# The first loads of x and W1: six loads of 128 to 256 KB, x on one queue and W1 on the other, in place of twelve of 64 to 128 KB

## The chip, the core and the metric

One core of one Trainium2 chip runs the whole kernel. The metric is the device time of one execution in microseconds (us), lower is better. The kernel before takes 141.57 us in the median of 13 runs, 140.27 us in the fastest and 144.7 us in the slowest.

A core has a matmul engine (PE; its weight loads are listed apart as PEld), a vector engine (DVE), an activation engine (ACT), a general engine (POOL), and sixteen DMA engines that move data between DRAM and on-chip memory. A transfer is started by an instruction on a queue. This kernel uses two queues: that of SP, an engine that does nothing else, and that of ACT, whose own instructions stand in the same order as its transfers.

## The reference

A sequence x of 2048 rows by 448 columns (bf16) goes through two branches, and a gate mixes them.

```python
g = sigmoid((x * gate_w).sum(-1, keepdims=True))
# branch A: a diagonal complex state space model with 448 states
dt = exp(log_dt);  Lam_bar = exp(dt * Lam);  B_bar = ((Lam_bar - 1) / Lam)[:, None] * B
h_t = Lam_bar * h_(t-1) + B_bar @ x_t          # 2048 steps
a = 2 * real(C @ h_t) + x * Dskip
# branch B: a feed-forward layer, 448 -> 1792 -> 448
b = silu(x @ w1) @ w2
out = g * a + (1 - g) * b
```

## The kernel before

Two successive rows of x are read as one row of 896 columns, so the 2048 rows are 1024 even and 1024 odd rows. They are worked on in four chunks of 512 rows: chunk 0 and 1 hold even rows, chunk 2 and 3 odd ones. x is needed with its columns on the partitions (XT). For chunk 0, PE does the turning: `turn_x` (L487) transposes 128x128 blocks of XN into PSUM and `turned_x` (L495) has DVE copy them to XT. For the other chunks DMA transposes on the SP queue (L308 to L320) do it. 448 columns are three full blocks of 128 (j = 0, 1, 2) and a rest of 64.

W1 has 1792 columns, two halves of 896 that are worked on in pairs (c = 0 and 1). Each half is loaded in three column ranges, `CUT`: the first 384 columns, which serve the first six output blocks of chunk 0, then 256, then 256 more.

An explicit tracker (class `Tracker`) puts the instructions on each engine in the order in which the Python code calls it, and adds a semaphore wait wherever a named buffer was last written by another engine or a transfer. Every load has its own key, so a matmul waits for exactly the loads whose keys it lists, and each load counts as landed when all of its sixteen parts are. The order on each engine is fixed by hand.

The order of the loads before is below. Each x load of columns 0-255 is 64 KB (one block k of 128 rows), each W1 load of a j and a half is 96 KB.

| SP queue | ACT queue |
|---|---|
| x rows k=0, columns 0-255 | x rows k=1 |
| W1 j=0, half 0 | W1 j=0, half 1 |
| x rows k=2 | x rows k=3 |
| W1 j=1, half 0 | W1 j=1, half 1 |
| log_dt, Lambda_re (one row each) | Lambda_im, Dskip (one row each) |
| x columns 256-511, k=0,1 (128 KB) | x columns 256-511, k=2,3 (128 KB) |
| W1 j=2, half 0 | W1 j=2, half 1 |
| W1's last 64 rows, half 0 (112 KB) | the same, half 1 |
| W1 second range (192 KB), third range (192 KB), half 0 | the same, half 1 |
| DMA transposes of x and B, gate and skip rows, x, W2 (1568 KB) ... | ACT's own work |

What PE does at the start, in its order:

- 22 matmuls of ones (`warm`), then `turn_x` of j=0 and j=1 for k=0,1, then two more of ones
- `ffn1_first` (L425): six output blocks of chunk 0, one matmul at a time, j=0 for the left half of the columns, then the right half, then j=1, then j=2. It is a generator: after its fourth matmul `turn_x(0, 1)` comes, after the sixth `turn_x(1, 1)`, and after the second of j=1 `mm_cols` (L467), which turns the four parameter rows R0 to R3 into columns. DVE prepares these with `rd` (L463), and copies the result to PV, from which all the scan's coefficients come. Then the turning of j=2 and 3 follows, and the other eight matmuls of `ffn1_first`.
- `ffn1_rem` (L441): the 64 rest columns, three pairs of matmuls. ACT applies silu.
- from then on `pair` (helper `lanes`, L361 to L370, matmul at L366): two 64-row matmuls side by side, for W1's other columns, the other chunks and the input projection of the scan (BT, BR). The first such pair is output blocks 6 and 7 of chunk 0, which reads both halves of W1's second range.

Later, the scan needs the half-swap of a tile over partitions: `VE<-VE`, two transfers on the SP queue (L938). They stand behind the load of W2 there. DVE's L842 reads them, and PE waits for that result. `XR` (copies of the 64 rest columns to the other half of the partitions, `swap_xr`, L236) is written by DVE when the transposed odd rows of x have landed.

Of the kernel before, what the change touches and what calls it, by code (L numbers as in the profile page):

```python
# [151 lines left out]
def gated_mix(nc, A_x, A_Lambda_re, A_Lambda_im, A_B_re, A_B_im, A_C_re, A_C_im, A_log_dt,  # L152
              A_Dskip, B_x, B_w1, B_w2, gate_w, out):
    with ExitStack() as ctx:
        E = ctx.enter_context
        T = Tracker(nc, ctx)

        def sb(name, shape, dtype):
            return E(nc.sbuf_tensor(name, list(shape), dtype))
# [5 lines left out]
        W1E = sb("W1E", [128, 4, F_FF], BF16)  # L165
# [24 lines left out]
        ID = sb("ID", [128, 128], BF16)  # L190
# [31 lines left out]
        ps = E(nc.psum_tensor("ps", [128, 8, 512], F32))  # L222
# [3 lines left out]
        def ld(eng, dst, src, key, group=None):  # L226
            return T.dma(eng, lambda e: e.dma_start(dst, src), writes=[key], group=group)  # L227
# [24 lines left out]
            return v.rearrange("(o n) -> o n", o=1)  # L252

        XH = XN[:, 0:8 * D].rearrange("p (k c) -> p k c", k=4)
        XA = ["XA0", "XA1", "XA2", "XA3", "XB0", "XB1"]
        HF = F_FF // 2
        CUT = ((0, 384), (384, 640), (640, HF))
        x0 = x2[0:512, 0:512].rearrange("(k p) c -> p k c", p=128)

        def ld_x(eng, k):  # L260
            ld(eng, XH[:, k, 0:256], x0[:, k, 0:256], XA[k])

        def ld_w(eng, j, c):
            f = slice(HF * c, HF * c + CUT[0][1])
            ld(eng, W1E[:, j, f], B_w1[j * 128:(j + 1) * 128, f], f"W1Ej{j}{c}")

        def ld_row(eng, i, v):
            ld(eng, R[i:i + 1, 0:D], row(v), f"R{i}", gR if i < 2 else gR2)
# [5 lines left out]
        def ld_wr(eng, c, f0, f1, key):  # L274
            ld(eng, W1E[64 * c:64 * c + 64, 3, f0:f1], B_w1[384:448, HF * c + f0:HF * c + f1], f"W1Er{key}{c}")

        for k, eng in enumerate(("sp", "act")):
            ld_x(eng, k)
        ld_w("sp", 0, 0)
        ld_w("act", 0, 1)  # L280
        for k, eng in ((2, "sp"), (3, "act")):
            ld_x(eng, k)
        ld_w("sp", 1, 0)
        ld_w("act", 1, 1)
        for i, (eng, v) in enumerate((("sp", A_log_dt), ("sp", A_Lambda_re), ("act", A_Lambda_im), ("act", A_Dskip))):
            ld_row(eng, i, v)
        for i, eng in enumerate(("sp", "act")):
            ld(eng, XH[:, 2 * i:2 * i + 2, 256:512], x0[:, 2 * i:2 * i + 2, 256:512], XA[4 + i])
        for c, eng in enumerate(("sp", "act")):
            ld_w(eng, 2, c)  # L290
        for c, eng in enumerate(("sp", "act")):
            ld_wr(eng, c, 0, HF, "")
        for c, eng in enumerate(("sp", "act")):
# [18 lines left out]
        for i, src in enumerate((A_B_re, A_B_im)):  # L312
# [17 lines left out]
             writes=["IOTA"])  # L330
# [9 lines left out]
        def nxt():  # L340
            n_bank[0] += 1
            return BANKS[(n_bank[0] - 1) % len(BANKS)]
# [56 lines left out]
        def ff(fb):  # L399
            return fb // 2 + NFB // 2 * (fb % 2)  # L400

        def wj(fb):
            i, c = fb // 2, fb % 2
            return [f"W1Ej{j}{c}" for j in range(3)] if i < 3 else [f"W1E1{c}"] if i < 5 else [f"W1E2{c}"]

        def w1(fb):
            return lambda p, j: W1E[p, j, ff(fb) * 128:(ff(fb) + 1) * 128] if j < 3 else \
# [10 lines left out]
        def ffn1_pair(c, fb, p=None):  # L418
            odd, h = c // 2, c % 2
            banks = at(p) if p is not None else [nxt(), nxt()]  # L420
            return (*[(banks[i], odd, h, w1(fb + i)) for i in range(2)],
                    wj(fb) + wj(fb + 1) + (XO if odd else XE)[h][0], rem_ffn1(odd, h, fb),
                    lambda: ffn1_act(c, fb, banks[0], 2))

        def ffn1_first():  # L425
            banks = [nxt() for _ in range(NF1)]
            for j, h in ((0, 0), (0, 1), (1, None), (2, None)):
                c = slice(0, 512) if h is None else slice(256 * h, 256 * h + 256)
                for n, fb in enumerate((0, 2, 4, 1, 3, 5)):
                    bank = banks[fb]  # L430
                    T.op("pe", lambda pe, fb=fb, bank=bank, j=j, h=h, c=c: pe.matmul(
                        ps[:, bank, c], W1E[:, j, ff(fb) * 128:(ff(fb) + 1) * 128], XT[:, j, c],
                        start=(h == 0), stop=(h == 0), skip_group_check=(h != 0)),
                        reads=[f"W1Ej{j}{fb % 2}"] + (
                            ["XTe02"] if j == 2 else [f"XTe0{j}{h}"] if h is not None else [f"XTe0{j}0", f"XTe0{j}1"]),
                        writes=[f"ps{bank}"])
                    if (j, h, n) in ((0, 0, 3), (0, 0, 5), (1, None, 1), (1, None, 3)):
                        yield
            yield banks
# [16 lines left out]
        def ffn1(c, f0=0, ahead=None):  # L456
            for fb in range(f0, NFB, 2):
                pair(*ffn1_pair(c, fb))
                if ahead and fb == 8:
                    ahead()  # L460
                yield
# [22 lines left out]
        PB = (6, 7, 6, 7)  # L484
        xp = [ps[:, b, 0:256].bitcast(BF16) for b in PB]

        def turn_x(j, i):  # L487
            def mm(pe):
                ins = None
                for k in (2 * i, 2 * i + 1):  # L490
                    ins = pe.transpose(xp[j][:, k * 128:(k + 1) * 128], XH[:, k, j * 128:(j + 1) * 128], ID[:, :])
                return ins
            T.op("pe", mm, reads=(XA[2 * i:2 * i + 2] if j < 2 else [XA[4 + i]]) + ["ID"], writes=[f"ps{PB[j]}"])

        def turned_x(j, i=None):  # L495
            c, key = (slice(0, 512), f"XTe0{j}") if i is None else (slice(256 * i, 256 * i + 256), f"XTe0{j}{i}")
# [2 lines left out]
        for j in range(2):  # L499
            turn_x(j, 0)  # L500
            turned_x(j, 0)
        warm(2, 5)
        first = ffn1_first()
        next(first)
        turn_x(0, 1)
        turned_x(0, 1)
        next(first)
        turn_x(1, 1)
        turned_x(1, 1)
        rd()  # L510
# [4 lines left out]
            reads=["ps7"], writes=["PV"])  # L515
# [37 lines left out]
        for j in (2, 3):  # L553
# [12 lines left out]
            reads=["f2"] + SGN, writes=["f2s"])  # L566
# [6 lines left out]
             reads=["li"] + SGN, writes=["lis"])  # L573
# [42 lines left out]
        def xblock(b):  # L616
            v = XN[:, 4 * b * D:4 * (b + 1) * D].rearrange("p (k c) -> p k c", k=4) if b > 1 else \
                XH[:, :, b * D:(b + 1) * D]
            return v, [*(XA if b < 2 else []), *([f"XN{b // 2}"] if b else [])]

# [12 lines left out]
        def skip():  # L633
            for b in range(4):
# [16 lines left out]
             writes=["BTz"] + BTK[2:4])  # L651
# [455 lines left out]
        f = ffn1(2)  # L1107
# [75 lines left out]
def bass_gated_mix__ssm_conv_s5__dense_activation_silu__prompt_kernel(nc, *args):  # L1183
    gated_mix(nc, *args)
# [28 lines left out]
```

## Time and profile before

The profiled execution took 141.06 us: a span of 139.3 us from the first instruction to the last, and 1.76 us around it. The median of the runs (141.57 us) is 0.51 us above it.

| | |
|---|---|
| profiled execution | 141.06 us |
| its span | 139.3 us |
| PE busy | 133.4 us, 96% |
| DVE busy | 114.7 us, 82% |
| ACT busy | 93.7 us, 67% |
| POOL busy | 13.6 us, 10% |
| moved by DMA | 11.94 MB, mean 86 GB/s |

When the first loads were issued and when they had landed, from the trace's records of each load's semaphore (us from the span's start; first and last of the sixteen parts):

| load | SP: issued, landed | ACT: issued, landed |
|---|---|---|
| x k=0 / k=1 | 0.79, 2.37 to 2.81 | 0.79, 2.57 to 2.98 |
| W1 j=0 | 1.23, 3.10 to 3.61 | 1.25, 3.44 to 3.84 |
| x k=2 / k=3 | 1.71, 3.68 to 4.16 | 1.74, 3.89 to 4.33 |
| W1 j=1 | 2.17, 4.39 to 5.06 | 2.22, 4.66 to 5.26 |
| two parameter rows | 2.65, 5.80 (last) | 2.71, 5.99 (last) |
| x columns 256-511 | 3.30, 5.33 to 6.80 | 3.59, 5.76 to 7.27 |
| W1 j=2 | 3.76, 6.14 to 7.54 | 4.03, 6.43 to 8.06 |
| W1 last 64 rows | 4.26, 6.87 to 8.32 | 4.56, 7.17 to 9.32 |
| W1 second range | 4.88, 8.45 to 10.90 | 5.12, 9.09 to 11.35 |
| W1 third range | 5.50, 9.68 to 12.27 | 5.86, 12.12 to 12.54 |

How to read the profile: a line of the timeline gives start, duration, engine, source line, operation, output<-input, and in brackets how long the engine had been idle before it and what ended that. A line of the chain gives start, duration and what the last work of the kernel was waiting for at that time. Line 366 and line 227 are helpers: all pair matmuls and all plain loads carry them.

### The profile page before, as it was taken

How to read it: one execution, taken by the hardware profiler on the slowest of the kernel's cores; microseconds unless marked ns; L12 is line 12 of the kernel's file. 1: busy time of each engine (PE TensorE's matmuls, PEld its weight loads, DVE VectorE, ACT ScalarE, POOL GpSimd, SP SyncE). 2: the span in 40 equal slices, each digit the busy share in tenths (PEclk: the TensorE clock that was granted, in tenths of full speed). 3: DMA queues.
4: the chain of work that ended last, by engine and by line, in shares of the span. 5: the costliest groups of instructions: out<-in, count | busy, mean ns of one | idle time of the engine just before them, and what ended most of it. 6: DMA issues, size and time to landing. Idle time of an engine off the chain costs nothing.

```text
span 139.3 us, 2417 instructions
## 1 busy us (share of the span) xinstructions
PE 133.4 (96%) x963; PEld 66.8 (48%) x963; DVE 114.7 (82%) x150; ACT 93.7 (67%) x146; POOL 13.6 (10%) x32
## 2 busy tenths in 40 slices
PE   7997999989997999999999999999999999999992
PEld 7633555533442555444445544444555555555552
DVE  1389979338469999999999999999999999990563
ACT  0387699797948995199997997697312536879200
POOL 7119086004000000000000000000000000000000
DMA  4999956998988440000023000000000000222123
GB/s 110 230 255 184 159 109 85 234 157 291 375 197 151 102 92 0 0 5 0 18 57 80 0 0 0 0 5 0 0 0 0 0 5 0 99 91 74 66 99 99
DMA packets 25681, 11.94 MB, mean 86 GB/s; under 512 B 16580, under 2 KB 25160, under 8 KB 25672
## 3 DMA queue, kind: packets, MB, share of 16 engines
q1 hardware_dynamic: 23652, 10.70, 33.8%
q10 hardware_dynamic: 2020, 1.11, 3.0%
q8 instruction: 7, 0.11, 0.4%
q14 instruction: 2, 0.02, 0.0%
HBM read 5.51 MB, written 1.84 MB: 53 GB/s over the span
## 4 chain that ended last, share of the span: by engine, by line
PE 77%; DMA 10%; ACT 5%; ACTq 3%; DVE 2%; SPq 1%; issue 1%
PE ps L366 32%; PE ps L773 31%; PE ps L995 15%; DMA VE<-VE 5%; DMA W1E<-in_B_w_dram 4%; ACTq L227 3%; ACT ps L806 2%; ACT VE L804 1%; DVE HS L842 1%; ACT ps L825 1%; SPq L938 1%; ACT VE L822 1%; ACT AT L453 1%; DVE TMPS L1019 1%
## 5 line engine op out<-in xcount | busy, mean ns | idle before, releaser
L773 PE MATMUL ps<-W,AT 128*128 128x448 bf16 x224 | 42.9, 353 | 0.0
L366 PE MATMUL ps<-XT,W1E 64*128 64x512 bf16 x325 | 40.1, 377 | 2.0 <-DMA W1E<-in_B_w_dram 1.1
L453 ACT ACTIVATE AT<-ps 128x1024 bf16<-128x1024 f32 x28 | 28.2, 1018 | 12.0 <-PE ps L366 11.9
L773 PEld LDWEIGHTS ps<-W,AT 128*128 128x128 bf16 x224 | 21.6, 98 | 21.2 <-issue 0.4
L366 PEld LDWEIGHTS ps<-XT,W1E 64*128 64x128 bf16 x325 | 17.4, 94 | 21.1 <-DMA W1E<-in_B_w_dram 1.5
L366 PE MATMUL ps<-XT,BT 64*128 64x512 bf16 x156 | 20.4, 377 | 0.1
L786 ACT ACTIVATE BT<-ps,GT 128x448 bf16<-128x448 f32 x8 | 5.1, 633 | 13.1 <-PE ps L773 13.1
L366 PEld LDWEIGHTS ps<-XT,BT 64*128 64x128 bf16 x156 | 8.3, 94 | 9.3 <-DVE HS L842 0.6
L842 DVE SCALAR_TENSOR_TENSOR HS<-VE,P,ps 128x512 bf16<-128x512 bf16 (+1 forms) x13 | 9.6, 781 | 3.1 <-PE ps L366 1.9
L886 DVE TENSOR_TENSOR_SCAN G<-P,Q 128x1024 f32<-128x1024 f32 (+1 forms) x6 | 11.4, 1922 | 0.0
L995 PE MATMUL ps<-CO,VE 128*128 128x448 bf16 (+2 forms) x63 | 11.1, 332 | 0.0
L995 PE MATMUL ps<-CO,HS 128*128 128x448 bf16 x56 | 11.1, 353 | 0.0
L366 PE MATMUL ps<-XR,W1E 64*128 64x512 bf16 x25 | 9.3, 377 | 0.0
L995 PEld LDWEIGHTS ps<-CO,VE 128*128 128x128 bf16 x63 | 6.0, 98 | 4.8
L995 PEld LDWEIGHTS ps<-CO,HS 128*128 128x128 bf16 x56 | 5.5, 98 | 5.1
L839 DVE TENSOR_TENSOR Q<-G,COS 128x2048 bf16<-128x2048 f32 (+1 forms) x4 | 7.0, 1756 | 0.1
L804 ACT ACTIVATE VE<-ps 128x1024 bf16<-128x1024 f32 x6 | 6.1, 1018 | 1.4 <-PE ps L366 1.3
L839 DVE TENSOR_TENSOR Q<-G,SIN 128x2048 bf16<-128x2048 f32 (+1 forms) x4 | 7.0, 1752 | 0.0
L806 ACT ACTIVATE ps<-VE,P 128x1024 f32<-128x1024 bf16 x6 | 6.7, 1119 | 0.2
L842 DVE SCALAR_TENSOR_TENSOR VE<-HS,P,FP 128x512 bf16<-128x512 bf16 (+1 forms) x7 | 6.6, 977 | 0.1
L1019 DVE SCALAR_TENSOR_TENSOR OT<-ps,GT,BT 128x448 bf16<-128x448 f32 x4 | 2.6, 682 | 4.8 <-PE ps L995 4.8
L842 DVE SCALAR_TENSOR_TENSOR FP<-HS,P,VE 128x1024 f32<-128x1024 bf16 (+1 forms) x4 | 6.2, 1550 | 0.1
(120 smaller groups left out, 169.8 us busy)
## 6 DMA issues: line engine op xcount, KB each, us to landing
W<-in_B_w_dram SPq DMA_DIRECT2D x1, 1568.0 KB, 10.7
XN<-in_A_x_dram SPq DMA_DIRECT2D x1, 896.0 KB, 5.7
out_dram<-OT SPq DMA_DIRECT2D x8, 112.0 KB, 1.7
out_dram<-TMPS SPq DMA_DIRECT2D x7, 112.0 KB, 1.7
HS<-HS SPq DMA_DIRECT2D x4, 128.0 KB, 2.5
W1E<-in_B_w_dram SPq DMA_DIRECT2D x2, 192.0 KB, 6.4
W1E<-in_B_w_dram ACTq DMA_DIRECT2D x2, 192.0 KB, 6.5
XN<-in_A_x_dram SPq DMA_DIRECT2D x1, 384.0 KB, 6.6
```

The costliest lines, as they stand in the source:

```text
L227: return T.dma(eng, lambda e: e.dma_start(dst, src), writes=[key], group=group)
L366: ins = pe.matmul(ps[:, bank, :], w(p, j), xh(odd, h, j, p), start=start and j == js[0], stop=stop and j == js[-1], skip_group_check=seeded)
L453: T.op("act", lambda e: e.activation(a[:, fb:fb + n, :], ps[:, bank:bank + n, :], AF.Silu), reads=[f"ps{bank + i}" for i in range(n)], wri ...
L773: ins = pe.matmul(ps[:, bank, 0:D], a[:, fb, q * 128:(q + 1) * 128], W2[:, ff(fb), :], start=(first and fb == 0), stop=(fb == NFB - 1), sk ...
L786: T.op("act", lambda e: e.activation(bs(tile), ps[:, bank, 0:D], AF.Copy, scale=sc), reads=[f"ps{bank}", "GT2" if h else "GRI"], writes=ks)
L804: T.op("act", lambda e: e.activation(VE[:, m:m + 2, hs], ps[:, b[0]:b[0] + 2, :], AF.Copy), reads=[f"ps{i}" for i in b], writes=vs)
L806: T.op("act", lambda e: e.activation(ps[:, o[0]:o[0] + 2, :], VE[:, m:m + 2, hs], AF.Copy, scale=c1("lr", pt)), reads=vs + ["lr"], writes= ...
L839: T.op("dve", lambda e: e.tensor_tensor(o, a, b, op), reads=reads, writes=writes)
L842: T.op("dve", lambda e: e.scalar_tensor_tensor(o, a, s, b, ALU.mult, ALU.add), reads=reads, writes=writes)
L886: T.op("dve", lambda e: e.tensor_tensor_scan(G[:, c, w], rb, Q1[:, c, w], init, ALU.mult, ALU.add), reads=[f"Q1{c}", "rr", f"G{c}"], write ...
L995: ins = pe.matmul(ps[:, bank, c], state(kt, odd, m), CO[:, m, c], start=False, stop=(m == YB[-1]), skip_group_check=True)
L1019: T.op("dve", lambda e: e.scalar_tensor_tensor(o, ps[:, bank, c], g, bs(tile)[:, c], ALU.mult, ALU.add), reads=[f"ps{bank}", "GT1_1", f"BS ...
```

## The change

The twelve loads of the first x block and of W1's first 384 columns per half become six.

- SP queue: x k=0,1 (columns 0-255, 128 KB); x k=2,3 (128 KB); x columns 256-511 of all four k (256 KB)
- ACT queue: W1 j=0, both halves in one load (192 KB); W1 j=1 (192 KB); W1 j=2 (192 KB)
- Then the four parameter rows, two on each queue as before. They stood behind the first eight loads and now stand behind all six.
- The loads after them are as before. The keys that the transposes and the matmuls wait for follow the loads: one for both halves of W1, one for all of x's columns 256-511.

The contiguous pieces are as before: 512 bytes of a row of x, 768 bytes of a row of W1. The instructions on PE, DVE and POOL and their order are the same. Each queue issues three first loads where it issued six.

```diff
-        XA = ["XA0", "XA1", "XA2", "XA3", "XB0", "XB1"]
+        XA = ["XA0", "XA1", "XB"]
...
-        def ld_x(eng, k):
-            ld(eng, XH[:, k, 0:256], x0[:, k, 0:256], XA[k])
-
-        def ld_w(eng, j, c):
-            f = slice(HF * c, HF * c + CUT[0][1])
-            ld(eng, W1E[:, j, f], B_w1[j * 128:(j + 1) * 128, f], f"W1Ej{j}{c}")
+        def ld_x(eng, i):
+            ld(eng, XH[:, 2 * i:2 * i + 2, 0:256], x0[:, 2 * i:2 * i + 2, 0:256], XA[i])
+
+        def ld_w(eng, j):
+            def head(v):
+                return v.rearrange("p (c f) -> p c f", c=2)[:, :, 0:CUT[0][1]]
+            ld(eng, head(W1E[:, j, :]), head(B_w1[j * 128:(j + 1) * 128, :]), f"W1Ej{j}")
...
-        for k, eng in enumerate(("sp", "act")):
-            ld_x(eng, k)
-        ld_w("sp", 0, 0)
-        ld_w("act", 0, 1)
-        for k, eng in ((2, "sp"), (3, "act")):
-            ld_x(eng, k)
-        ld_w("sp", 1, 0)
-        ld_w("act", 1, 1)
+        ld_x("sp", 0)
+        ld_w("act", 0)
+        ld_x("sp", 1)
+        ld_w("act", 1)
+        ld("sp", XH[:, :, 256:512], x0[:, :, 256:512], XA[2])
+        ld_w("act", 2)
         for i, (eng, v) in enumerate((("sp", A_log_dt), ("sp", A_Lambda_re), ("act", A_Lambda_im), ("act", A_Dskip))):
             ld_row(eng, i, v)
-        for i, eng in enumerate(("sp", "act")):
-            ld(eng, XH[:, 2 * i:2 * i + 2, 256:512], x0[:, 2 * i:2 * i + 2, 256:512], XA[4 + i])
-        for c, eng in enumerate(("sp", "act")):
-            ld_w(eng, 2, c)
         for c, eng in enumerate(("sp", "act")):
             ld_wr(eng, c, 0, HF, "")
...
-            return [f"W1Ej{j}{c}" for j in range(3)] if i < 3 else [f"W1E1{c}"] if i < 5 else [f"W1E2{c}"]
+            return [f"W1Ej{j}" for j in range(3)] if i < 3 else [f"W1E1{c}"] if i < 5 else [f"W1E2{c}"]
...
-                        reads=[f"W1Ej{j}{fb % 2}"] + (
+                        reads=[f"W1Ej{j}"] + (
...
-            T.op("pe", mm, reads=(XA[2 * i:2 * i + 2] if j < 2 else [XA[4 + i]]) + ["ID"], writes=[f"ps{PB[j]}"])
+            T.op("pe", mm, reads=[XA[i if j < 2 else 2]] + ["ID"], writes=[f"ps{PB[j]}"])
```

## The prediction

> **What bounds the kernel now.** First the chain of work that ended last, in order of time (start, duration, what; the ACT and SP steps that it passes between 26 and 34 us are left out):
>
> ```profile
> 5.12 6.22 DMA W1E<-in_B_w_dram
> 11.35 0.14 issue
> 11.48 14.65 PE ps L366 x134
> ...
> 34.65 7.02 DMA VE<-VE
> 41.66 0.03 issue
> 41.69 1.29 DVE HS L842
> 42.98 0.05 issue
> 43.03 2.33 PE ps L366 x20
> ```
>
> Two transfers set the pace: W1's second range lets the long run of pair matmuls start at 11.48, and the half-swap VE<-VE lets it go on at 43.03. After that, the table of busy time by stretch (length, then PE's busy time) has no room:
>
> ```profile
> 43.00:60.00 17.00, 16.97 (x114) 8.16 (x116) 16.76 (x22) 12.58 (x33) 0.00 (x0) 1.00 0.29 62
> 60.00:100.00 40.00, 40.00 (x305) 18.51 (x300) 39.52 (x38) 34.36 (x51) 0.00 (x0) 1.00 0.06 14
> 100.00:136.00 36.00, 36.00 (x194) 18.78 (x193) 29.66 (x37) 16.93 (x32) 0.00 (x0) 1.00 0.12 42
> ```
>
> So the time is the start at 43.03, plus 139.3 - 43.03 = 96.3 us that the change doesn't reach, plus the 1.76 us around the span. The timeline shows what comes before 43.03, and where an engine waits (in brackets) for a transfer:
>
> ```profile
> 6.08 0.17 DVE L464 COPY R<-R 4x64 bf16<-4x64 bf16 x1 [0.26 <-DMA R<-in_A_Dskip_dram]
> ...
> 6.64 0.24 PE L470 MATMUL ps<-ID,R 128*128 128x4 bf16 x4
> ...
> 11.48 1.02 PE L366 MATMUL ps<-XT,W1E 64*128 64x512 bf16 x7 [1.06 <-DMA W1E<-in_B_w_dram]
> ...
> 29.91 0.29 DVE L239 COPY XR<-XT 64x512 bf16<-64x512 bf16 x1 [3.57 <-DMA XT<-in_A_x_dram]
> ...
> 30.26 0.39 PE L366 MATMUL ps<-XR,BT 64*128 64x512 bf16 x1 [0.47 <-DVE XR L239]
> ...
> 41.69 1.28 DVE L842 SCALAR_TENSOR_TENSOR HS<-VE,P,ps 128x1024 bf16<-128x1024 bf16 x1 [1.20 <-DMA VE<-VE]
> ```
>
> The reader is to see three meeting points. At 11.48, 30.26 and 43.03 PE waits for transfers: 1.06, 0.47 and 0.91 us (the last is PE's wait for L842 in the table of waits). A late PE loses the last two before it loses time: **0.47 + 0.91 = 1.38 us of cover** behind 11.48. An early transfer chain gains at most the 0.91 us, since then PE itself is the bound. The transfers of the SP queue run one behind the other all this time: XTr0 (landing 29.89), W2 (issued 30.52, landed 41.17) and VE<-VE, which was issued by 34.65 and landed at 41.66 behind W2's stragglers. A shift of the first loads' end therefore goes through to 43.03, and a later issue of VE<-VE, within the 5 us that it queues behind W2, does not.
>
> **Removed: six loads.** Issuing one takes 0.42 us on its queue (0.39 to 0.47 in the timeline), 1.3 us for each queue. That is worth nothing: the last issues of first-stage loads end at 6.3 us, the data at 12.5, so the queues have a backlog. What a load costs the DMA engines is read from the records of single pieces. A 512-byte piece mostly takes 27 ns, one of 768 bytes 36 ns, one of 1792 bytes 74 ns. Above these bases the pieces of the twelve loads lose 11.2 us in total, 0.70 us per engine, often at the first pieces of a load. Half as many loads: **0 to -0.35 us**, if the loss goes with loads (0 if it goes with bytes). Besides, the engines were short of work in the first stretch: from 1.75 to 3.0 us they were busy 0.92 of 1.25 us, and some stood still from about 2.4 to 2.8, between the first load of a queue and its second. Longer first loads fill this: **0 to -0.2 us**. Bytes and piece sizes are unchanged, so nothing else gets cheaper.
>
> The Trainium skill's DMA: Bandwidth & Descriptors (Rules for kernel authors) would make more of it: it tells to coalesce small transfers, as under 64 KB one pays mostly overhead, and its section on the anatomy of a DMA puts about 2 us fixed cost on each (for GpSimd's path). As an estimate, six of twelve on two queues would be 6 us. The rows say otherwise: on SP the first four landed at 2.81, 3.61, 4.16 and 5.06, 0.55 to 0.90 us apart, so the fixed part overlaps. I take the rows.
>
> **Moved: who shares with whom.** The same page (Issuing engines are not separate DMA queues) says that loads of both queues run on the same sixteen engines and interleave. That rule speaks against the change: x's first 128 KB had the engines to themselves, and now W1's 192 KB run beside them. The piece records agree: SP's and ACT's pieces alternate about one for one. So I count pieces per engine, in the order of each queue. Before, each queue has 8 of x, 8 of W1, 8, 8, then 16 of x, 8 of W1, 4 long ones, 24, 24. After, SP has 16, 16, 32 of x, ACT 16, 16, 16 of W1, then as before. The start is 1.81 us.
>
> - First x half: 16 x pieces with about 9 of W1 beside them (SP started 0.2 us ahead) is 16 x 27 + 9 x 36 = 0.76 us of work in place of 16 x 27 = 0.43, so up to +0.33, less the idle gap of 0.2: landing at about 3.1 against 2.98. W1 j=0 stays near 3.8. The transposes hang on this, +0.1 us.
> - Second x half: 32 x and 25 W1 pieces, 1.76 us of work against 1.44 before; landing about 4.5 (4.33 before). PE is at `turn_x(0,1)` only at 4.82. Nothing lost.
> - W1 j=1 about 5.3 (5.26; used at 6.2), j=2 about 7.4 (8.06): covered.
> - x's other columns: SP's 64 pieces of x, and beside them ACT's 48 of W1, 4 long and 12 more: 64 x 27 + 48 x 36 + 4 x 74 + 12 x 27 = 4.1 us of work against 3.0 before. Landing: 1.81 + 4.1 plus the lateness of before (7.27 - 1.81 - 3.0 = 2.4) is 8.3, or scaled by (7.27 - 1.81)/3.0 it is 9.2.
> - **The parameter rows.** SP's two stand behind all that: 4.1 us of work where there were 2.0 (16 + 16 pieces on each queue). They landed 2.15 us later than 1.81 + 2.0; so now 8.1, or by proportion 1.81 + 4.1 x 4.18/2.0 = 10.3. I take 8.9, nearer the first, as with fewer loads the loss should shrink.
>
> What waits for the rows: DVE's `rd`, behind it the PV copy and the turned copies; PE's `mm_cols`, and behind that on PE everything up to the pair matmuls. From 6.9 PE has nothing to do. `mm_cols` can start some 0.3 us after the rows (0.65 before, with other work between): 9.2 against 6.64. Then PE needs 0.1 + 2 x 0.215 + 8 x 0.06 + 8 x 0.215 + 3 x 0.215 = 3.4 us (matmul spacings from the timeline): pairs could start at 12.6.
>
> The second range of W1 on SP: 92 pieces on each queue before it is through, 5.8 us of work against 5.3, less 0.2 to 0.55: 11.2 to 11.8 against 11.35. So PE's rows decide: start at about **12.6 against 11.48, +1.1 us; ends: rows at 8.1 give 11.8 (+0.3), at 10.3 give 14.0 (+2.5)**. +1.1 is inside the 1.38 us of cover.
>
> DVE's chain behind PV moves by 1.3 to 2 us; it has idle stretches of 0.30 us before the copy at 15.82, 0.57 before the BT copy at 20.05, 0.98 before L636 at 25.25, and 3.57 before 29.91. ACT's first tables need it at 19.31, 3 us after they could. Covered.
>
> **The sum.** End of the first loads: total work is equal; -0.55 to 0 from the above, and SP now has 16 more pieces than ACT in the rest of the stage, which ends up alone at 27 ns each: up to +0.43. Between these I take -0.2 us, near the middle. PE is just covered. Span 139.1, profiled execution 140.9; on the median, 141.57 - 0.2 = **141.4 us**. I call 0.5% (0.7 us) what a measurement of this kernel can tell from no change.
>
> **Rivals.**
> - *The rows come too late* (slower). One mechanism: PE stands before `mm_cols`. It decides when `mm_cols` starts after 9.5 (9.5 + 3.4 = 11.48 + 1.38), and costs beyond it one for one: rows at 10.3 give 2.5 - 1.38 = +1.1, 142.7 us. A second rule bears here: TensorE: Matmul & The Clock Gate (Part 1) says that about 3.4 us of idleness halves PE's clock. The row speaks for no loss: PE stood still from 10.3 to 11.48 and the next pairs came 0.21 us apart. But now it stands still for 2.3 to 3.7 us. With the gate the 3.4 us behind `mm_cols` would take up to twice as long, and the time would be up to 144. For it: PE and DVE take all in order. Against: 1.38 us of cover. 0.30.
> - *The stage ends later* (slower): SP's surplus lasts, stalls on single pieces (some up to 1 us in the records) fall on it; transposes, W2 and VE<-VE move by +0.8: 142.4. Against: equal bytes. 0.10.
> - *Fewer loads pay in full* (faster): the stage ends 0.8 to 0.9 earlier, as the slowest engine gains more than the mean; PE must not be late by over 0.5. Capped by 0.91: 140.7. For it: the second range landed over 2.3 us from first to last part, so stragglers set it. 0.25.
> - *Nothing reaches 43.03 beyond noise*: the forecast's case, 0.35; its own range 140.9 to 142.0.
>
> **The numbers.** Faster 0.25, same 0.35, slower 0.30 + 0.10 = 0.40. Range: down to 140.6 (the cap), up to 143.0, which takes in rows at 10.3 and leaves the halved clock out.
>
> **What would show it.** In the profile after: the wait of `rd` for the rows ends at 8 to 9 (6.08 before), `mm_cols` near 9; x's first half not earlier than 2.9; PE's wait before the pairs gone or put to the rows; waits at 30.26 and 43.03 shrunk by a late PE; 43.03 itself within 0.5 us. Rows landing before 7.5 would make the interleaving count wrong; a start at 43.03 moved with PE still waiting there would mean that the transfer chain moved, and no PE stall.

## The result and the profile after

The changed kernel takes 139.88 us in the median of 11 runs (139.11 to 140.98), before 141.84 us in the 48 runs beside it. The ratio is 0.9914, with a 95% interval of 0.9884 to 0.9945: faster by 0.9%. A second series gave 139.76 us against 141.49 us and a ratio of 0.9953 (0.9905 to 1.0001). The ratio leaves out every run that is over 1.5% above the fastest of its kernel, which cuts the upper part of the wide spread of before (139.8 to 144.7 us, and one run of 496 us), so the medians over all runs lie further apart (1.2 to 1.4%) than the ratios.

So the sign of the likeliest case was right, though for another reason than the one it gave; its size (-0.2 us) was not, and 139.88 us lies below the range that was given. The case that came is the third rival: the fewer loads pay.

The profiled execution doesn't show it at first sight: 141.18 us, a span of 139.4 us, as long as the one of before and longer than any of the 11 timed runs. Where it spends this is in its chain of work that ended last (start in us, duration, what):

```profile
10.67 0.76 PE ps L440 x6
11.42 22.17 PE ps L361 x204
33.60 0.02 issue
33.62 1.03 ACT VE L799
34.65 0.49 SPq L933
35.14 0.04 issue
35.19 6.62 DMA VE<-VE
41.80 0.03 issue
41.83 1.29 DVE HS L837
43.12 0.05 issue
43.16 2.33 PE ps L361 x20
```

(Lines are five lower than before: 366 is 361, 842 is 837.) The first transfer on the chain of before, W1's second range, is gone from it: the pairs follow PE's own work, and run on for 22 us without another meeting point. The half-swap is still there, and landed at 41.80. W2, ahead of it on the queue, had 15 of its 16 parts landed by 39.21 and the last at 41.19. The timeline at the three meeting points and at the rows:

```profile
7.01 0.17 DVE L459 COPY R<-R 4x64 bf16<-4x64 bf16 x1 [0.36 <-DMA R<-in_A_Dskip_dram]
...
7.69 0.24 PE L465 MATMUL ps<-ID,R 128*128 128x4 bf16 x4
...
11.26 1.02 PE L361 MATMUL ps<-XT,W1E 64*128 64x512 bf16 x7
...
29.18 0.29 DVE L239 COPY XR<-XT 64x512 bf16<-64x512 bf16 x1 [3.64 <-DMA XT<-in_A_x_dram]
...
29.52 0.39 PE L361 MATMUL ps<-XR,BT 64*128 64x512 bf16 x1
...
41.83 1.28 DVE L837 SCALAR_TENSOR_TENSOR HS<-VE,P,ps 128x1024 bf16<-128x1024 bf16 x1 [2.50 <-DMA VE<-VE]
43.16 0.39 PE L361 MATMUL ps<-XT,W1E 64*128 64x512 bf16 x2 [1.78 <-DVE HS L837]
```

The line of before that goes with the last of these is:

```profile
43.03 0.39 PE L366 MATMUL ps<-XT,W1E 64*128 64x512 bf16 x2 [0.91 <-DVE HS L842]
```

The reader is to see that two brackets on PE have gone: the 1.06 us at 11.48 and the 0.47 us at 30.26. The third has grown from 0.91 to 1.78 us. PE itself came to the half-swap at 43.16 - 1.78 = 41.38, against 43.03 - 0.91 = 42.12 before: **0.74 us earlier**. Of this 0.22 is the earlier start of the pairs (11.26 for 11.48) and 0.47 the wait at 30.26; 0.05 is left over. In this one execution the half-swap gave it all back. With no wait at 43 the span would have been 139.4 - 1.78 = 137.6, and with 1.76 us around it 139.4 us, within the timed runs (139.1 to 141.0) and 0.5 us below their median.

### The profile page after: what moved, and what is told of

It reads as the page before. It is cut to its first block, busy times and chain, and to the rows that moved or that the text cites. A ratio compares the mean times of both kernels' runs of the same rounds, so it can differ in the third digit from the quotient of the medians.

```text
span 139.4 us, 2409 instructions
## 1 busy us (share of the span) xinstructions
PE 134.0 (96%) x963; PEld 65.9 (47%) x963; DVE 114.6 (82%) x150; ACT 93.7 (67%) x146; POOL 15.3 (11%) x32
## 4 chain that ended last, share of the span: by engine, by line
PE 88%; DMA 7%; DVE 2%; ACT 1%; SPq 0%; issue 0%
PE ps L361 37%; PE ps L768 31%; PE ps L990 15%; DMA VE<-VE 5%; PE ps L426 4%; DMA XN<-in_A_x_dram 2%; PE ps L486 1%; DVE HS L837 1%; ACT VE L799 1%; DVE TMPS L1014 1%; PE ps L440 1%; SPq L933 0%; PE ps L474 0%; PE ps L465 0%
## 5 line engine op out<-in xcount | busy, mean ns | idle before, releaser
L361 PEld LDWEIGHTS ps<-XT,W1E 64*128 64x128 bf16 x325 | 16.5, 94 | 21.7 <-DVE HS L837 2.3
```

Source lines behind the costliest of these rows:

```text
L361: ins = pe.matmul(ps[:, bank, :], w(p, j), xh(odd, h, j, p), start=start and j == js[0], stop=stop and j == js[-1], skip_group_check=seeded)
```

## The experiments

Each kernel ran beside before, in three series, in which before had medians of 141.49, 142.02 and 141.13 us; a ratio always goes with the before of its own series. All of them compute the whole reference.

### The changed kernel again, and its rows moved ahead

> The changed kernel once more, as the measure for the runs beside it. Theory A (the first stage of transfers ends earlier, and with it the pairs' start, XTr0 and the half-swap): ratio to before 0.989 to 0.994 again, span about 138.0. Theory B (chance: the runs of before that the ratio stands on were unlucky): 0.996 to 1.003.

139.76 us, ratio 0.9953 (0.9905 to 1.0001). By the ratio alone chance is not shut out here; by the other series (0.9914, interval below 1) and by the kernels below it is. In its profile the rows landed at 6.85 and the pairs started at 11.01.

```diff
         ld_x("sp", 1)
         ld_w("act", 1)
-        ld("sp", XH[:, :, 256:512], x0[:, :, 256:512], XA[2])
-        ld_w("act", 2)
         for i, (eng, v) in enumerate((("sp", A_log_dt), ("sp", A_Lambda_re), ("act", A_Lambda_im), ("act", A_Dskip))):
             ld_row(eng, i, v)
+        ld("sp", XH[:, :, 256:512], x0[:, :, 256:512], XA[2])
+        ld_w("act", 2)
```

> The changed kernel with the rows moved ahead of x's other columns and W1's j=2. If late rows cost the changed kernel something: rows land near 6, pairs start 0.3 to 0.5 earlier than 11.26, ratio to before 0.986 to 0.989. If they are covered: the same as the changed kernel, about 0.991. If small one-engine loads in front disturb the stage: 0.993 to 0.998.

140.35 us, ratio 0.9962 (0.9911 to 1.0012). The rows landed at 4.95 and the pairs started at 10.87, 0.39 and 0.14 us earlier than in the two profiles of the changed kernel, and it is no faster. In this profile PE waits 1.38 us for the half-swap, so the earlier start is lost there. The ratio can't tell covered rows from a small cost of the moved rows: it falls into the band that was expected for such a cost, but so does the 0.9953 of the changed kernel beside it.

### The arrangement without the merging

The twelve loads of before, x's six on SP and W1's six on ACT, the rows behind them.

```diff
-        for k, eng in enumerate(("sp", "act")):
-            ld_x(eng, k)
-        ld_w("sp", 0, 0)
-        ld_w("act", 0, 1)
...
+        for i in range(2):
+            for k in (2 * i, 2 * i + 1):
+                ld_x("sp", k)
+            for c in range(2):
+                ld_w("act", i, c)
+        for i in range(2):
+            ld("sp", XH[:, 2 * i:2 * i + 2, 256:512], x0[:, 2 * i:2 * i + 2, 256:512], XA[4 + i])
+        for c in range(2):
+            ld_w("act", 2, c)
         for i, (eng, v) in enumerate((("sp", A_log_dt), ("sp", A_Lambda_re), ("act", A_Lambda_im), ("act", A_Dskip))):
             ld_row(eng, i, v)
...
```

> The twelve loads of before, but x on SP, W1 on ACT and the rows behind them, as after: the arrangement without the merging. If the number of loads is what pays: ratio near 1.000 (0.997 to 1.003), the second range of W1 landing near 11.3 as before. If the arrangement pays: ratio near 0.991, as the changed kernel. If the arrangement costs and the merging pays more: 1.003 to 1.008.

141.44 us, ratio 1.004 (0.9996 to 1.0084): the arrangement doesn't pay, if anything it costs. PE's waits in its profile, from the table of waits (who, for whom, us in total, times, longest):

```profile
PE ps L363 <- DMA XT<-in_A_x_dram: 1.6, 1, 1.6
PE ps L363 <- DVE HS L839: 0.5, 1, 0.5
PE ps L363 <- DMA W1E<-in_B_w_dram: 0.4, 1, 0.4
```

All three meeting points are back, the one at 30 us the largest. (There PE waits for the transposed odd rows themselves, the transfer ahead of XTr0 on the queue, which landed at 30.48.)

### The merging with another arrangement

```diff
         ld_x("sp", 0)
         ld_w("act", 0)
-        ld_x("sp", 1)
-        ld_w("act", 1)
+        ld_w("sp", 1)
+        ld_x("act", 1)
```

> The six loads of the changed kernel with x and W1 crossed: SP takes x k=0,1, W1 j=1, x's other columns, ACT takes W1 j=0, x k=2,3, W1 j=2; the rows behind. If merging alone pays: as the changed kernel, 139.6 to 140.1. If one tensor per queue matters as well: 140.6 to 141.5.

139.74 us, ratio 0.9907 (0.9874 to 0.9941), the same as the changed kernel. So **it is six loads in place of twelve, and not one tensor per queue**: the six pay in either arrangement, and the twelve don't pay in the new one. PE's waits for transfers at 11 and 30 us are gone as in the changed kernel; it waits for x's second block (landed at 5.85) and little at 43:

```profile
PE ps L486 <- DMA XN<-in_A_x_dram: 1.0, 2, 0.7
PE ps L474 <- PEq L1193: 0.8, 1, 0.8
PE ps L361 <- DVE HS L837: 0.3, 1, 0.3
```

### Half of the merging

x in three loads with W1 in six, and W1 in three with x in six; x on SP and W1 on ACT, rows behind.

x merged, W1 not (against the changed kernel):

```diff
         def ld_w(eng, j):
-            def head(v):
-                return v.rearrange("p (c f) -> p c f", c=2)[:, :, 0:CUT[0][1]]
-            ld(eng, head(W1E[:, j, :]), head(B_w1[j * 128:(j + 1) * 128, :]), f"W1Ej{j}")
+            for c in range(2):
+                f = slice(HF * c, HF * c + CUT[0][1])
+                ld(eng, W1E[:, j, f], B_w1[j * 128:(j + 1) * 128, f], f"W1Ej{j}{c}")
...
```

W1 merged, x not:

```diff
         def ld_x(eng, i):
-            ld(eng, XH[:, 2 * i:2 * i + 2, 0:256], x0[:, 2 * i:2 * i + 2, 0:256], XA[i])
+            for k in (2 * i, 2 * i + 1):
+                ld(eng, XH[:, k, 0:256], x0[:, k, 0:256], XA[k])
...
-        ld("sp", XH[:, :, 256:512], x0[:, :, 256:512], XA[2])
+        for i in range(2):
+            ld("sp", XH[:, 2 * i:2 * i + 2, 256:512], x0[:, 2 * i:2 * i + 2, 256:512], XA[4 + i])
...
```

(The keys that the matmuls and transposes wait for follow the loads again.)

> x in three loads on SP, W1 still in six on ACT, nine in all; order as in the changed kernel. If the number of loads pays in proportion: half way between the twelve by queue (median 141.4) and the six (139.8), 140.5 to 140.8, ratio 0.997 to 1.001. If it is ACT's queue (six issues of W1 in a row) that matters: no better than the twelve, 141.2 to 141.6.

> W1 in three loads on ACT, x still in six on SP, nine in all. If in proportion: 140.5 to 140.8. If W1's merging is what pays: as the changed kernel, 139.6 to 140.0, ratio 0.991 to 0.996; if x's: as the twelve by queue, 141.2 to 141.6.

142.14 us, ratio 1.005 (1.001 to 1.0091), and 142.26 us, ratio 1.0051 (1.0009 to 1.0093). By the ratios both are slower than before: nothing is in proportion to the number of loads, and both medians lie above every range that was expected. With x merged it is the rows, as its chain shows:

```profile
4.47 5.08 DMA R<-in_A_Dskip_dram
9.55 0.04 DVEq L146
9.58 0.05 issue
9.63 0.18 DVE R L459
9.81 0.14 issue
9.95 0.24 PE ps L465 x4
```

and the timeline of the same kernel:

```profile
9.95 0.24 PE L465 MATMUL ps<-ID,R 128*128 128x4 bf16 x4 [2.72 <-DVE R L459]
...
13.52 0.82 PE L361 MATMUL ps<-XT,W1E 64*128 64x512 bf16 x6
```

This is the slower rival of the prediction, in another kernel: PE stands 2.72 us before the column matmuls, the pairs start 2.04 us after those of before, the waits at 30 and 43 are used up (PE waits for no transfer any more after the start), and the rest shows in the time. The last row is one of ACT's, whose list is the longer one: when its piece started, at 8.67, 1691 pieces of SP's 512-byte loads had started ahead of it, where it had been 1022 in the changed kernel. SP's later loads had run past ACT's list.

With W1 merged it is not the rows. PE waits for x's block k=3, which stands fourth in SP's longer list and landed at 7.30, and then for nothing up to the pairs; the rows landed at 8.84, in time for the column matmuls at 10.38:

```profile
7.44 0.37 PE L488 MATMUL ps<-ID,XN 128*128 128x128 bf16 x2 [1.46 <-DMA XN<-in_A_x_dram]
```

The pairs start at 14.01, 2.53 us after those of before.

### Half of the merging, with the rows ahead

The same two kernels, with the move of the rows shown above.

> x in three loads, W1 in six, with the four rows moved ahead of x's other columns and W1's j=2. Theory R (with nine loads it is the rows, landing at 9.55, that hold PE beyond its cover: columns at 9.95, pairs at 13.5): rows land at 5 to 6, pairs start at 11 to 11.5, median 140.0 to 140.8, ratio 0.993 to 1.000. Theory T (nine loads lose elsewhere, in the transfers' chain): still 141.8 to 142.4, ratio near 1.005, with PE waiting at 30 or 43.

> W1 in three loads, x in six on SP, the rows moved likewise. Here PE had waited for x's block k=3 (7.30) and then for the rows (8.84). Theory R: if the rows are what costs, pairs near 11.5 and a median of 140.0 to 140.8; if x's block is late by itself, pairs at 12 to 12.5 and 140.6 to 141.4; Theory T: 141.8 to 142.4.

x merged: 141.22 us, ratio 0.9985 (0.995 to 1.002), so by the ratios 0.9 us better than with the rows behind, and still no faster than before. Theory R is right in part. What is left is in the timeline:

```profile
12.97 0.82 PE L361 MATMUL ps<-XT,W1E 64*128 64x512 bf16 x6 [1.47 <-DMA W1E<-in_B_w_dram]
```

The rows landed at 6.28, and now the pairs wait for the half of W1's second range that ACT loads: issued at 5.12 and landed at 12.84, where SP's had been issued at 3.54 and landed at 9.76. ACT has nine loads in this stage to SP's six, and SP's transposes, issued from 4.69, run beside ACT's last loads. That the longer list falls behind, and that the transposes hold it up further, is a reading of this profile; no run deals nine loads out evenly.

W1 merged: 141.83 us, ratio 1.0052 (1.0019 to 1.0085), against the expectation of theory R. The rows landed at 5.52, but the column matmuls came at 8.62 all the same and the pairs at 12.20, as x's first blocks were in only at 4.22 and PE waited before it turned them. That is a 0.72 us later start of the pairs than in before, which should be covered, and the span of this profile is that of before, 139.3 us. So it doesn't explain the loss of 0.7 us that the ratio shows; what costs there stays open. The theory had misread the run with the rows behind, in which PE did not wait for the rows.

### Late rows in before

```diff
         ld_w("act", 1, 1)
-        for i, (eng, v) in enumerate((("sp", A_log_dt), ("sp", A_Lambda_re), ("act", A_Lambda_im), ("act", A_Dskip))):
-            ld_row(eng, i, v)
         for i, eng in enumerate(("sp", "act")):
             ld(eng, XH[:, 2 * i:2 * i + 2, 256:512], x0[:, 2 * i:2 * i + 2, 256:512], XA[4 + i])
         for c, eng in enumerate(("sp", "act")):
             ld_w(eng, 2, c)
+        for i, (eng, v) in enumerate((("sp", A_log_dt), ("sp", A_Lambda_re), ("act", A_Lambda_im), ("act", A_Dskip))):
+            ld_row(eng, i, v)
```

> Before, with the four parameter rows moved behind W1's j=2 loads and nothing else. Theory of the prediction (late rows hold PE, with 1.38 us of cover behind): rows at 7.5 to 8.5, the column matmuls at 8 to 9, the pairs near 12; ratio 0.998 to 1.003 as it is covered. If rows on one engine in the midst of the loads hold that engine up and with it the stage, moving them pays: 0.993 to 0.997. If the cover isn't there: 1.004 to 1.010.

140.79 us, ratio 0.9994 (0.9935 to 1.0053). The rows landed at 8.15, and the timeline has what the prediction had expected of the changed kernel:

```profile
8.24 0.17 DVE L464 COPY R<-R 4x64 bf16<-4x64 bf16 x1 [2.48 <-DMA R<-in_A_Dskip_dram]
...
8.55 0.24 PE L470 MATMUL ps<-ID,R 128*128 128x4 bf16 x4 [1.82 <-DVE R L464]
...
12.12 1.02 PE L366 MATMUL ps<-XT,W1E 64*128 64x512 bf16 x7
```

The pairs start 0.64 us late, PE's wait at 30 is gone and the one at 43 has shrunk to 0.2, and the span is no longer than that of before (138.6 us): **the cover is real** in this profile, and with x merged, 2.04 us late, it is used up. The ratio agrees, but could hide a loss of up to 0.7 us. The profile also shows 8.55 + 3.57 = 12.12, so the 3.4 us that PE needs from the column matmuls to the pairs were well sized. They were no longer after the 1.82 us of waiting, nor after the 2.72 us with x merged (9.95 to 13.52, 3.57 again). No wait of PE here reached the 3.4 us of the rule on the clock in the prediction, so that rule is not tested.

### The half-swap moved ahead of a long load

In before and in the changed kernel, the 896 KB load of x's second half moves on SP from ahead of W2 to behind the half-swap.

```diff
         ldt(XT[:, 7:8, 512:1024], x2[512:1024, 768:896], "XTr1")
-        load_xn(1)
...
         def load_c():
+            load_xn(1)
             gC = T.group()
```

> Before, with the 896 KB load of x's second half (its values are read from 45.5 us on) moved on SP from ahead of W2 to behind the half-swap. Theory A (the half-swap behind W2 is what sets the start at 43): VE<-VE lands 2 to 4 us earlier, PE's wait before 43 is gone, the rest is PE's own arrival at 42.1: ratio 0.990 to 0.994, and the spread of the runs shrinks. If PE's arrival is the bound in most runs: 0.998 to 1.002.

> The same move in the changed kernel. Theory A1 (the change works by way of PE's earlier arrival, 41.4 against 42.1 in the two profiles): it stays 0.6 to 0.8 us faster than before with the move, ratio 0.984 to 0.988. Theory A2 (the change works by way of an earlier half-swap alone): both are equal once the meeting point at 43 is gone, 0.990 to 0.994.

Before with the move: 140.30 us, ratio 0.9956 (0.9907 to 1.0006), between its two expectations, the half-swap landing at 39.22 for 41.66. The changed kernel with the move: 139.37 us, ratio 0.9881 (0.982 to 0.9942), landing at 37.66 for 41.80. In both profiles PE no longer waits at 43. The change is still worth 0.93 us by the medians and 0.75% by the two ratios (0.9881 / 0.9956), about what it is worth without the move. That speaks for theory A1: with the half-swap out of the way, **PE's own earlier arrival keeps about the whole gain**. It rests on the times alone, of 12 and 6 runs, and the intervals of the two ratios overlap; the two profiled executions differ by only 0.15 us (spans 137.64 and 137.49), though the pairs start at 11.33 and 10.70.

In the kernel without the move, an earlier arrival is not enough by itself. The run of 139.88 us had a span of 138.1 us, so PE went on there at 138.1 - 96.3 = 41.8, and the half-swap's result had come by then, 1.2 us before the 43.03 in the profile of before. The four profiles of six loads that keep the x load in front have the half-swap landing at 40.11 to 41.80, those of twelve at 40.92 to 42.34. So the half-swap, too, seems to come earlier in most runs of the changed kernel; by how much is not shown. PE's waits after its first work in the changed kernel with the move:

```profile
PE ps L485 <- DMA XN<-in_A_x_dram: 0.3, 1, 0.3
PE ps L360 <- DVE XR L239: 0.2, 1, 0.2
```

> The changed kernel with the 896 KB load of x behind the half-swap and the rows early: neither the rows nor the half-swap should hold PE. If both waits were still worth something in most runs: median 138.6 to 139.1, ratio 0.979 to 0.985. If PE's own work is the bound: as with the late x load alone, 139.2 to 139.5, ratio about 0.988.

139.63 us, ratio 0.9894 (0.9862 to 0.9926), no better than without the early rows. The time is the one that was expected if PE's own work is the bound, but the profile doesn't show that: PE waits again before the pairs, 0.53 us for W1's second range (landed at 11.09), and they start at 11.22 for 10.70. The changed kernel with the late x load is the fastest of all that ran by the median and by the ratio, though the intervals of it and of the changed kernel overlap.

## Why the prediction was wrong in its size

The three meeting points, PE's order behind the rows and the cover were read rightly. That the rows would hold PE was not. Each size in its turn:

| | before | predicted | measured (first, second profile) |
|---|---|---|---|
| x's first 128 KB landed | 2.98 | 3.1 | 3.54, 3.02 |
| W1 j=2 landed | 8.06 | 7.4 | 7.20, 7.33 |
| x's other columns landed | 7.27 | 8.3 to 9.2 | 6.95, 7.03 |
| last row landed | 5.99 | 8.9 | 6.92, 6.85 |
| column matmuls | 6.64 | 9.2 | 7.69, 7.25 |
| W1's second range landed, the later half | 11.35 | 11.2 to 11.8 | 10.37, 10.87 |
| pairs start | 11.48 | 12.6 | 11.26, 11.01 |
| half-swap landed | 41.66 | 41.5 | 41.80, 41.21 |

**The step that failed is the landing of the rows and of x's other columns.** The prediction counted 4.1 us of work ahead of the rows and added the lateness of before (2.15 to 2.4 us), or scaled by it. Of its two ends for the rows, 8.1 and 10.3 us, even the lower is 1.2 us above the measured 6.9. Both terms were too large (slips such as 10.3 for 1.81 + 4.1 x 4.18/2.0 = 10.4 change nothing):

- *The work ahead.* When the piece of the last row started (5.98 and 5.83 us), pieces worth 3.6 and 3.5 us had started, at the prediction's own 27, 36 and 74 ns. The pieces of the two queues do not alternate one for one, as the prediction read from the records of before: in the first profile 172 of SP's loads started to 7 of ACT's from 2.0 to 2.5 us, and 578 to 123 from 6.0 to 8.0 us. Rows before 7.5 us were the prediction's own sign that this count would be wrong.
- *The lateness.* It came to 1.5 and 1.6 us. The stalls of the first loads' pieces, which are a part of it, were 0.30 and 0.43 us per engine in the two profiles, 0.70 before. But one profile was a poor base: over four profiles of twelve loads the loss is 0.41 to 0.70 us, over six of six loads 0.28 to 0.47, so the gain is some 0.14 us in the mean, and single profiles differ by more.

The other half of the price, 0.2 us for filling the first gap, did not come: of the pieces that started from 1.75 to 3.0 us the engines had 0.89 us of work (0.91 in the second profile) against 0.92.

From this the rest follows. With the rows at 6.9 PE isn't 1.1 us late but 0.2 early, as W1's second range lands before PE comes to it. So the 1.38 us of cover had nothing to cover, and its first part, the wait at 30, turned into gain: XTr0 landed at 29.15 and 29.27 for 29.89.

**The reason for the cap at 43 was wrong too.** The prediction took the 96.3 us behind 43.03 as fixed (right: it is 96.3 us after as well), and said that an earlier half-swap gains at most 0.91 us, as PE's arrival stays where it is. But the arrival moves with the change. It is the floor below the meeting point: 41.38 and 41.56 in the two profiles of the changed kernel, 41.2 with the mixed six, 42.1 in before and with late rows, 43.2 with the twelve by queue (where it includes the wait at 30). Floor + 96.3 + 1.76 gives 139.4, 139.6, 139.3, 140.2 and 141.3 us; the medians are 139.9, 139.8, 139.7, then 141.1 to 142.0 for before and 140.8 for late rows, and 141.4. Those of before stand 0.9 us and more above its floor, as in its profile, where the wait at 43 is 0.91 us. So the change moved the floor by 0.6 to 0.7 us, and this counts in a run only when the half-swap is in time.

The first rival's price could be seen in two other kernels. With x merged the pairs start 2.04 us late, 0.66 us beyond the cover; the ratio of 1.005 is 0.7 us (0.1 to 1.3), and the profiled spans differ by 0.3 us. With W1 merged they start 2.53 us late, 1.15 beyond it; the ratio is 0.7 us again, and the spans differ by 0.8. So the sum holds roughly.

The second rival didn't come. The later half of W1's second range landed at 9.98 to 11.09 in six profiles of six loads and at 10.36 to 11.35 in four of twelve, some 0.5 us earlier in the mean. The stalls explain 0.14 of it. A rival that no run separates is the time on the queues: with three first loads to issue in place of six, this half was issued at 4.35 to 4.47 us, in the twelve at 5.09 to 5.12, 0.7 us later. The prediction put that at nothing because the queues have a backlog. Whether it is the rest stays open.

## What to carry to other kernels

Where an engine meets several transfers one after another, find its own arrival at each (start less wait) and not only the start, and ask whether the change moves both. Merge early loads on all queues alike: here three long loads on one queue beside six short ones on the other lost all that merging won. And size a landing in a busy stage from the stalls of several profiles: those of like kernels ran from 0.41 to 0.70 us.

## What the runs showed of the hardware that was not expected

- A queue with a longer list of loads falls behind the other. Each row stood behind the same 64 pieces per engine on SP or 48 on ACT, and the last one landed at 6.9 us with three loads on each queue, at 9.55 us with three on SP and six on ACT; 1022 and 1691 of SP's 512-byte pieces had started ahead of it.
- Stalls of single pieces, 0.1 to over 1 us where 27 to 36 ns is usual, make up 0.28 to 0.70 us per engine for the first loads in ten profiles of six and twelve loads, and 0.51 to 1.07 us in four of nine. They change from profile to profile of like kernels.
- Of a load of W1 with two runs per row the issue took 0.63 to 0.65 us in the changed kernel's profile, of one with one run 0.42 to 0.49 us in that of before; of x with 256 pieces it took 0.45.
- PE standing still for 2.72 us didn't lengthen the matmuls that followed: 3.57 us from the column matmuls to the pairs, after a wait of 1.82 us, of 2.72 us, or of none (7.69 to 11.26 in the changed kernel).
